# Splitting the first activation load and moving one residual add from TensorE to VectorE in a transformer block

## The chip, the cores and the metric

The kernel runs on one core of one Trainium2 chip. The metric is the device time of one execution in microseconds; several executions are timed and the median is given. The profile's span is about 1.7 us shorter than the timed execution, and spans are compared only with spans. The engines are TensorE (PE in the profile, its weight loads PEld), VectorE (DVE), ACT, GpSimd (POOL) and SP, whose queue issues 46 of the 50 transfers of the kernel before.

## The reference, cut to what matters

```python
x = A_x                                   # 2048 x 512, bf16
xn = _layernorm(x)                        # per row
# A: 32 heads of 16, causal attention over a window of 256 keys; then @ wo
# B: ((xn @ w_gate) * (xn @ w_up)) @ w_down, inner width 1792
return x + A(xn) + B(xn)
```

The sum of the three terms is the point: attention's output projection and the down projection accumulate in the same bank of PSUM, the memory that this kernel's matmuls write to, and the residual x is added last. Copying a finished bank out of PSUM is called evacuating it.

## The kernel before

Rows are worked off in four chunks of 512 (T = 0 to 3), each of four blocks of 128 rows. The first chunk is loaded and normalised ahead of everything:

```python
        for lo, hi in ((0, 1), (1, 4)):                      # x blocks 0, then 1 to 3
            nc.sync.dma_start(out=self.x[:, lo:hi, :], in_=xv[:, lo:hi, :])
        for lo in (1024, 512, 0):                            # V, K, Q thirds
            nc.sync.dma_start(out=self.Wqkv[:, :, lo:lo + 512], in_=wq[:, :, lo:lo + 512])
        ...
        for _ in range(38):                                  # the author's warm-up; no run isolates it
            nc.tensor.matmul(wps[:], lhsT=ident[:], rhs=ident[:], start=True, stop=True)
```

The rest is one hand-made list scheduler. Attention proceeds in groups of scores; between the groups "fillers" (all the dense matmuls, in pairs) are emitted until a running count of cost reaches the group's share of the total:

```python
        total = sum(w[0] for w in work) - RESERVE + SCORES * len(steps) + VALUES * (len(due) - 1)
        ...
        for g, s in enumerate(steps):
            fill(-1, g)
            self.scores(*s)                   # matmuls, then ACT's exponential, then GpSimd's masks
            ...
            upto = total * (g + 1) / len(steps)
            ...
                fill(upto, g)                 # fillers until the share is used up
                self.mask_diag(*s)
```

Every `scores` ends with up to four masks on GpSimd, which need the exponential. And a filler without matmuls, of cost 0, prepares a new chunk's V tile on GpSimd:

```python
    def new_chunk(self, T):
        ...
        nc.gpsimd.memset(self.heads(self.V[T])[:, :, :, 16:18], 1.0)   # the column of ones
        nc.gpsimd.memset(self.V[T][:, VW - 16:], 0.0)
        nc.gpsimd.memset(self.VS[T][:, SW - 16:], 0.0)

        def project(T):                       # in the list of fillers
            add(0, lambda: self.new_chunk(T))
            for b in range(4):
                for ks in halves:
                    add(2, lambda t=4 * T + b, ks=ks: self.proj_v(t, ks), ...)
```

The softmax here doesn't subtract the row's maximum and nothing guards it: scores larger than these inputs give would overflow.

## Time and profile before

| What | Before |
|---|---|
| time, median of 3 | 268.93 us |
| span of the profile | 267.5 us |
| TensorE busy | 258.4 us, 97% |
| VectorE, ACT, GpSimd busy | 68%, 64%, 43% |
| second norm statistics start | 4.80 us |
| first V projection matmul | 7.49 us |
| last evacuation on VectorE starts | 263.79 us |

The timeline of the kernel before at the start, with the last evacuation as its end; columns are start, length (both us), engine, line, operation, tiles, count, and in brackets the idle time before it and what ended it.

```profile
2.86 0.69 DVE L148 BATCH_NORM_STATS2 st<-x 128x6 f32<-128x512 bf16 x1 [1.02 <-DMA x<-in_A_x_dram]
4.80 0.70 DVE L148 BATCH_NORM_STATS2 st<-x 128x6 f32<-128x512 bf16 x1 [0.84 <-DMA x<-in_A_x_dram]
7.49 0.81 PE L200 MATMUL vp<-Wqkv,xnT 128*128 128x512 bf16 x3
263.79 0.56 DVE L402 TENSOR_TENSOR y<-L,x 128x384 bf16<-128x384 f32 x1 [2.47 <-PE L L384]
```

VectorE waits 0.84 us for blocks 1 to 3. Everything else in the norm follows in VectorE's order, so the wait is paid once by the whole kernel: in the chain that ended last, the load's 3.52 us (from 1.25 us) are followed by VectorE's norm work and from 8.43 us by TensorE. The count x3 stands for four matmuls: 22 matmul records are missing, so counts and busy time of TensorE are a little low.

### The profile page before, as it was taken

How to read it: one execution, taken by the hardware profiler on the slowest of the kernel's cores; microseconds unless marked ns; L12 is line 12 of the kernel's file. 1: busy time of each engine (PE TensorE's matmuls, PEld its weight loads, DVE VectorE, ACT ScalarE, POOL GpSimd, SP SyncE). 2: the span in 40 equal slices, each digit the busy share in tenths (PEclk: the TensorE clock that was granted, in tenths of full speed). 3: DMA queues.
4: the chain of work that ended last, by engine and by line, in shares of the span. 5: the costliest groups of instructions: out<-in, count | busy, mean ns of one | idle time of the engine just before them, and what ended most of it. 6: DMA issues, size and time to landing. Idle time of an engine off the chain costs nothing.

```text
span 267.5 us, 8861 instructions
## 1 busy us (share of the span) xinstructions
PE 258.4 (97%) x3860; PEld 119.1 (45%) x3882; DVE 181.7 (68%) x352; ACT 170.6 (64%) x132; POOL 113.8 (43%) x281
## 2 busy tenths in 40 slices
PE   6899999999999999999999999999999999999994
PEld 6444434444444444444444444444444444434453
DVE  4377898958756859676674868857762575978251
ACT  2675658696556776769656676668765667665500
POOL 5215333422674533345556433545444353443500
PEclk9999999999999999999999999999999999999999
DMA  6999911120023000001014100000200010000002
GB/s 205 373 358 334 250 22 22 23 47 0 4 61 81 20 2 4 2 2 44 5 23 97 43 0 5 0 4 2 44 5 20 26 39 2 2 0 2 4 2 81
DMA packets 19336, 15.13 MB, mean 57 GB/s; under 512 B 7264, under 2 KB 19296, under 8 KB 19296
## 3 DMA queue, kind: packets, MB, share of 16 engines
q1 hardware_dynamic: 18464, 14.09, 18.1%
q8 instruction: 30, 0.49, 0.7%
q10 hardware_dynamic: 832, 0.46, 0.6%
q14 instruction: 10, 0.08, 0.1%
HBM read 9.70 MB, written 2.10 MB: 44 GB/s over the span
## 4 chain that ended last, share of the span: by engine, by line
PE 88%; DVE 7%; issue 1%; DMA 1%; ACT 1%; SPq 0%; POOL 0%; DVEq 0%; POOLq 0%
PE up L359 17%; PE gp L345 17%; PE psd L378 16%; PE qkp L212 11%; PE S L261 9%; PE acc L316 6%; PE psd L384 5%; PE vp L200 4%; PE L L378 2%; DMA x<-in_A_x_dram 1%; DVE hT L363 1%; DVE st L148 1%; DVE at L322 1%; DVE gsb L353 1%; DVE xn L168 1%
## 5 line engine op out<-in xcount | busy, mean ns | idle before, releaser
L268 ACT ACTIVATE P<-S 128x2048 bf16<-128x2048 f32 x76 | 141.0, 1855 | 57.4 <-PE S L261 49.9
L137 POOL TENSOR_SCALAR_AFFINE_SELECT P<-P 64x256 bf16<-64x256 bf16 x224 | 97.3, 434 | 128.9 <-ACT P L268 118.2
L345 PE MATMUL gp<-xnT,Wg 128*128 128x512 bf16 x224 | 60.0, 380 | 0.1
L359 PE MATMUL up<-xnT,Wu 128*128 128x512 bf16 x224 | 59.6, 380 | 0.0
L378 PE MATMUL psd<-Wd,hT 128*128 128x512 bf16 (+1 forms) x198 | 48.7, 368 | 1.4 <-issue 1.3
L363 DVE TENSOR_TENSOR hT<-up,gsb 128x512 bf16<-128x512 f32 x56 | 38.4, 686 | 16.0 <-PE up L359 14.4
L289 DVE TENSOR_TENSOR P<-P,diag 128x512 bf16<-128x512 bf16 (+1 forms) x76 | 30.6, 404 | 10.4 <-ACT P L268 10.4
L322 DVE STREAM_TRANSPOSE at<-acc 128x512 f32<-128x512 f32 x30 | 19.7, 695 | 19.7 <-PE acc L316 19.7
L378 PEld LDWEIGHTS <-hT 128*128 128x128 bf16 x238 | 21.6, 98 | 25.3 <-issue 2.6
L359 PEld LDWEIGHTS <-Wu 128*128 128x128 bf16 x224 | 20.4, 98 | 25.3 <-issue 2.5
L345 PEld LDWEIGHTS <-Wg 128*128 128x128 bf16 x224 | 20.3, 98 | 25.5 <-issue 2.7
L261 PE MATMUL S<-Q,K 16*64 16x320 bf16 (+1 forms) x720 | 31.2, 260 | 0.4
L261 PE MATMUL S<-Q,Ko 32*64 32x320 bf16 (+1 forms) x720 | 31.1, 260 | 0.0
L212 PE MATMUL qkp<-xnT,Wqkv 128*128 128x512 bf16 x128 | 30.0, 380 | 0.0
L261 PEld LDWEIGHTS <-K 16*64 16x64 bf16 x720 | 12.2, 103 | 32.2 <-issue 32.2
L353 DVE CAST gsb<-gp 128x512 bf16<-128x512 f32 x36 | 24.5, 681 | 2.6 <-PE gp L345 1.3
L351 ACT ACTIVATE gsb<-gp 128x512 bf16<-128x512 f32 x20 | 11.9, 597 | 11.8 <-PE gp L345 11.1
L316 PE MATMUL acc<-P,VS 64*32 64x320 bf16 (+4 forms) x672 | 18.9, 254 | 0.0
L316 PE MATMUL acc<-P,V 64*32 64x320 bf16 (+4 forms) x672 | 18.4, 254 | 0.1
L212 PEld LDWEIGHTS <-Wqkv 128*128 128x128 bf16 x128 | 11.7, 98 | 14.5 <-issue 1.4
L384 PE MATMUL psd<-Wo,OT 128*128 128x512 bf16 (+1 forms) x55 | 15.5, 368 | 0.6 <-issue 0.6
L316 PEld LDWEIGHTS <-V 64*32 64x32 bf16 x720 | 14.5, 90 | 2.8 <-issue 2.4
(55 smaller groups left out, 194.1 us busy)
## 6 DMA issues: line engine op xcount, KB each, us to landing
Wg<-in_B_w_gate_dram SPq DMA_DIRECT2D x2, 896.0 KB, 10.4
Wu<-in_B_w_up_dram SPq DMA_DIRECT2D x2, 896.0 KB, 13.0
Wd<-in_B_w_down_dram SPq DMA_DIRECT2D x1, 1792.0 KB, 17.3
out_dram<-y SPq DMA_DIRECT2D x14, 128.0 KB, 1.8
Wqkv<-in_A_wqkv_dram SPq DMA_DIRECT2D x3, 512.0 KB, 6.4
x<-in_A_x_dram SPq DMA_DIRECT2D x1, 1024.0 KB, 10.9
VS<-V SPq DMA_DIRECT2D x6, 144.0 KB, 2.6
x<-in_A_x_dram SPq DMA_DIRECT2D x1, 512.0 KB, 11.4
```

Of the source, the lines that this page charges most:

```text
L137: nc.gpsimd.affine_select(out=v, in_=v, pattern=pattern + [[1 if diag else -1, 64]], compare_op=ALU.is_ge if diag else ALU.is_gt, fill=0.0 ...
L212: nc.tensor.matmul(ps[:], lhsT=self.Wqkv[:, k, lo:lo + 128], rhs=self.xnT[T][:, :, k, :], start=(k == 0), stop=(k == 3))
L261: nc.tensor.matmul(S[64 * par:64 * par + 64, e, col:col + n], lhsT=(self.Ko if par else self.K)[U][rows, c, keys], rhs=self.Q[T][rows, c, ...
L268: nc.scalar.activation(out=P[:, :, 0:col], in_=S[:, :, 0:col], func=ACT.Exp, scale=0.25)
L289: self.nc.vector.tensor_tensor(out=v, in0=v, op=ALU.min, in1=self.diag.unsqueeze(1).unsqueeze(1).to_broadcast([128, 4, n, 64]))
L316: nc.tensor.matmul(accs[par][32 * e:32 * e + 32, q:q + n], lhsT=v, rhs=P[rows, e, col:col + n], start=(i == 0), stop=(i == len(todo) - 1), ...
L345: nc.tensor.matmul(ps[:], lhsT=self.Wg[:, k, 128 * f:128 * f + 128], rhs=self.xnT[T][:, :, k, :], start=(k == 0), stop=(k == 3))
L353: nc.vector.tensor_copy(out=self.gsb[:], in_=ps[:])
L359: nc.tensor.matmul(ps[:], lhsT=self.Wu[:, k, 128 * f:128 * f + 128], rhs=self.xnT[T][:, :, k, :], start=(k == 0), stop=(k == 3))
L363: nc.vector.tensor_tensor(out=self.hT[T][:, f, :], in0=ps[:], in1=self.gsb[:], op=ALU.mult)
L378: nc.tensor.matmul(ps, lhsT=self.hT[T][:, f, 128 * b:128 * b + 128], rhs=self.Wd[:, f, c0:c1], start=(f == 0), stop=False)
L384: self.nc.tensor.matmul(ps, lhsT=self.OT[T][:, c, 128 * b:128 * b + 128], rhs=self.Wo[:, c, c0:c1], start=False, stop=(c == 3))
```

## The change

The intent has two parts. At the front, x block 1 gets its own transfer, so that its norm need not wait for 384 KB. At the end, the last chunk's second block no longer receives its x by an identity matmul and a copy on ACT; VectorE adds x while it evacuates the bank, as for most other blocks.

```diff
-        for lo, hi in ((0, 1), (1, 4)):
+        for lo, hi in ((0, 1), (1, 2), (2, 4)):
             nc.sync.dma_start(out=self.x[:, lo:hi, :], in_=xv[:, lo:hi, :])
@@ the last chunk's fillers
             if b < 3:
                 wo(T, b, (0, 1, 2))
-            if b in (1, 3):
-                add(1, lambda b=b: self.add_x(T, b, 0 if b == 1 else 1))
+        add(1, lambda: self.add_x(T, 3, 1))
@@ the tail
             self.wo(T, b, (3,))
-            self.store(T, b, on_act=(b == 1))
+            self.store(T, b)
```

## The prediction

> **What bounds the kernel now.** TensorE. The page gives PE 258.4 us busy of a 267.5 us span (97%), against DVE 68%, ACT 64%. The table of busy time by stretches shows PE at 9.6 to 10.0 of every 10 us from 10 to 260 us, at full granted clock. The exceptions are both ends. In the chain of waits the first large piece is the load of x blocks 1 to 3 (from 1.25 us, 3.52 us), then VectorE's norm work; only from 8.43 us is the chain TensorE's. At the end PE stops at 263.8 us; evacuation, store and closing take 3.5 us.
>
> **Front.** The timeline shows x block 0 landing at 2.85 us (2.0 us after issue) and VectorE through with its statistics at 3.95 us, then idle 0.84 us until blocks 1 to 3 (384 KB) land and the second statistics start at 4.80 us. The later norms follow in VectorE's order. After the change block 1 (128 KB) is issued at 1.2 us and, at block 0's 2.0 us, lands near 3.3 us. [...] Second statistics can start at 3.97 us, 0.83 us earlier; the third at 5.1 us if blocks 2 and 3 have landed. The same 512 KB passes, so I estimate 4.7 to 5.1 us: hardly a wait. Weights are issued 0.4 us later: the V third of Wqkv (issue 1.72 us, landing 4.5 us later, at 6.2) would come by 6.2 to 6.6 us; the first V matmul, now at 7.49 us, wants it at 6.65. The other weights have slack. TensorE's unbroken stretch begins 0.6 to 0.85 us earlier and keeps that. Estimate: 0.7 us.
>
> **End.** One 128x512 identity matmul goes: 0.216 us in an unbroken stream (four merged span 1.03 us, one alone 0.379). It lies on a full engine: 0.2 us. The add moves to VectorE, 0.68 us instead of ACT's 0.60, where VectorE is idle from 261.3 to 263.8 us: its three stores are done by 262.1 us, before the last evacuation. Four stores issue on SP instead of three, 0.4 us each, also done in time. No cost.
>
> **Moved without appearing in the diff.** One filler fewer lowers the scheduler's total, so from the second chunk on some pairs of matmuls cross a scores group and some evacuations change engine (gate copies on ACT 20 to 21, on VectorE 36 to 35; K copies on ACT 4 to 3). On engines at 64 to 68% I take this as noise of up to 0.3 us either way. [...]
>
> **Prediction.** 268.93 - 0.7 - 0.2 = 268.0 us, range 267.6 to 268.5. Faster by over 2%: 1%; within 2%: 98.5%; slower: 0.5%.
>
> **What would show each step.** Second statistics at about 4.0 us with hardly a wait for x; third at 5.1 us; first V matmul at 6.7 us; QK projection at 10.9 to 11.1 us instead of 11.74; PE's last matmul at about 262.9 us; no ACT store at 260 us; the tail after it still 3.5 us.
>
> **What would make it wrong.** Blocks 2 and 3 landing after 5.3 us, or Wv after 6.7 us: front gain 0.3 us or less. Reordered fillers opening waits of TensorE on scores or PSUM banks: the gain is eaten. The VectorE store delaying the last evacuation: a wait before the 128x384 store.

0.7 us for the front and 0.2 us for the end, 268.93 - 0.7 - 0.2 = 268.03 us, given as 268.0.

## More of the kernel before

```profile
181.14 2.76 PE L200 MATMUL vp<-Wqkv,xnT 128*128 128x512 bf16 x11
181.19 0.33 POOL L118 MEMSET V<- 128x256 bf16 x1
181.34 1.88 ACT L268 ACTIVATE P<-S 128x2048 bf16<-128x2048 f32 x1 [1.16 <-PE S L261]
183.12 1.57 ACT L204 ACTIVATE V<-vp 128x512 bf16<-128x512 f32 x3
183.29 1.99 POOL L137 TENSOR_SCALAR_AFFINE_SELECT P<-P 64x256 bf16<-64x256 bf16 x4 [1.68 <-ACT P L268]
184.55 1.91 ACT L268 ACTIVATE P<-S 128x2048 bf16<-128x2048 f32 x1
185.07 1.89 PE L212 MATMUL qkp<-xnT,Wqkv 128*128 128x512 bf16 x8
```

The memset at 181.19 us is done long before ACT's first copy of V at 183.12 us, and TensorE goes from V's projection to scores and on to the Q and K projection without a wait.

`proj_v` takes one of four rotating PSUM banks (`ps_m`), and ACT copies the result into V, behind the memset. The score tile S has one buffer only.

## The result, and the profile after

The changed kernel takes 270.29 us (median of 4, 270.00 to 270.41), the kernel before 268.96 us in the same rounds. The ratio is 1.005 (95% interval 1.0033 to 1.0067). Ratios here are taken over the fast runs of the same rounds, so they are not quite the ratio of the medians quoted. 1.3 us were lost where 0.9 us were to be gained, a miss of 2.3 us. That the forecast "within 2%" held says little: any loss of less than 5 us would have met it.

The front did what was intended. Timeline of the changed kernel at the start:

```profile
3.89 0.68 DVE L148 BATCH_NORM_STATS2 st<-x 128x6 f32<-128x512 bf16 x1
5.01 0.69 DVE L148 BATCH_NORM_STATS2 st<-x 128x6 f32<-128x512 bf16 x1
6.93 0.88 PE L200 MATMUL vp<-Wqkv,xnT 128*128 128x512 bf16 x3
```

The second statistics start at 3.89 us with no wait for x, and the first V matmul 0.56 us earlier. The loss must lie later. The list of what TensorE waited for, of the changed kernel (instruction and line, what it waited for, then us in total, times, longest), finds it:

```profile
PE qkp L212 <- ACT V L204: 1.2, 1, 1.2
PE S L261 <- ACT P L268: 0.9, 1, 0.9
```

Neither line is in that list of the kernel before. Each wait happened once. The busy time by stretches shows where: the columns are the stretch, its length, then busy time and instruction count of PE, PEld, DVE, ACT and POOL, the granted clock, the DMA share and GB/s. First the kernel before:

```profile
180.00:192.00 12.00, 11.95 (x127) 4.98 (x127) 8.87 (x18) 9.88 (x11) 5.64 (x15) 1.00 0.12 26
```

Then the changed kernel:

```profile
180.00:192.00 12.00, 9.88 (x117) 4.20 (x118) 6.07 (x11) 8.36 (x9) 4.73 (x13) 1.00 0.12 26
```

TensorE lost 2.07 us here, at full clock. The timeline of the changed kernel in that stretch:

```profile
180.41 2.76 PE L200 MATMUL vp<-Wqkv,xnT 128*128 128x512 bf16 x11
180.61 1.88 ACT L268 ACTIVATE P<-S 128x2048 bf16<-128x2048 f32 x1 [0.72 <-PE S L261]
182.55 2.09 POOL L137 TENSOR_SCALAR_AFFINE_SELECT P<-P 64x256 bf16<-64x256 bf16 x4 [2.59 <-ACT P L268]
184.70 0.33 POOL L118 MEMSET V<- 128x256 bf16 x1
185.06 1.57 ACT L204 ACTIVATE V<-vp 128x512 bf16<-128x512 f32 x3 [2.57 <-POOL V L118]
185.71 1.89 PE L212 MATMUL qkp<-xnT,Wqkv 128*128 128x512 bf16 x8 [1.21 <-ACT V L204]
186.51 1.90 ACT L268 ACTIVATE P<-S 128x2048 bf16<-128x2048 f32 x1
188.46 0.30 PE L261 MATMUL S<-Q,K 16*64 16x256 bf16 x4 [0.86 <-ACT P L268]
```

Read it as a chain. The memset now stands behind four masks in GpSimd's queue, and those wait for an exponential that ends at 182.49 us. GpSimd is not busy before that: it idles 2.59 us, with a ready memset behind a mask that is not (in the run early_memset below GpSimd runs no memset between 175 and 190 us: it is done before, so its buffer is free by then). The masks take 2.09 us, the memset runs at 184.70 instead of 181.19 us, and ACT's copies of V begin at 185.06 instead of 183.12 us. By then V's projections, whose last matmul ends at 184.50 us, hold all four banks of `ps_m`, so TensorE waits 1.21 us for the first to come free. The next exponential stands behind three copies in ACT's queue and starts 1.96 us later than before (186.51 against 184.55 us); as S has one buffer, TensorE waits another 0.86 us for it.

Neither engine let a ready instruction pass in this trace: GpSimd idled 2.59 us ahead of the masks with the memset behind them, and ACT idled 2.57 us ahead of the copies of V with the exponential behind them, whose scores had ended by 183.53 us.

Why did the memset move? The removed identity matmul was a filler of cost 1. Without it `total` is lower by 1, every group's share `upto` a little lower, and at one boundary the cost-0 filler `new_chunk` no longer fits before the scores, but only after them. Working the scheduler's sums through shows how narrow it was: the cost spent so far was 754.55 in both kernels, against a share of 754.62 before the change and 753.92 after it. The built instruction order of GpSimd confirms it. Before:

```
TensorScalarAffineSelect P_3663   (x2)
Memset V3      <- here
Memset V3, Memset VS3
TensorScalarAffineSelect P_3817   (x4, wait for the exponential)
```

After, with other buffer numbers:

```
TensorScalarAffineSelect P_3661   (x2)
TensorScalarAffineSelect P_3810   (x4, wait for the exponential)
Memset V3      <- here
Memset V3, Memset VS3
```

At the end, the three full-width stores on VectorE and the four transfers on SP cost nothing: the last evacuation waits for TensorE alone, as before. It comes at 265.14 us:

```profile
265.14 0.56 DVE L402 TENSOR_TENSOR y<-L,x 128x384 bf16<-128x384 f32 x1 [1.87 <-PE L L384]
```

The sum closes. From the first V matmul to this evacuation the kernel before took 263.79 - 7.49 = 256.30 us, the changed one 265.14 - 6.93 = 258.21 us: 1.91 us more, which is the 2.07 us of waits less 0.2 us for the identity matmul, within 0.1 us.

### The profile page after: what moved, and what is told of

Read it like the earlier page. It is cut to its first block, busy times and chain, and to the rows that moved or that the text cites. A ratio compares the mean times of both kernels' runs of the same rounds, so it can differ in the third digit from the quotient of the medians.

```text
span 268.7 us, 8864 instructions
## 1 busy us (share of the span) xinstructions
PE 259.0 (96%) x3860; PEld 119.5 (44%) x3881; DVE 182.2 (68%) x353; ACT 170.0 (63%) x131; POOL 113.7 (42%) x281
## 4 chain that ended last, share of the span: by engine, by line
PE 87%; DVE 6%; issue 2%; ACT 1%; POOL 1%; DMA 1%; POOLq 0%; DVEq 0%
PE up L359 17%; PE gp L345 16%; PE psd L378 16%; PE qkp L212 10%; PE S L261 9%; PE acc L316 6%; PE psd L384 5%; PE vp L200 4%; PE L L378 2%; DVE hT L363 1%; DVE st L148 1%; POOL P L137 1%; DVE gsb L353 1%; DMA x<-in_A_x_dram 1%; DVE at L322 1%
## 5 line engine op out<-in xcount | busy, mean ns | idle before, releaser
L353 DVE CAST gsb<-gp 128x512 bf16<-128x512 f32 x35 | 23.9, 682 | 3.0 <-PE gp L345 2.0
L351 ACT ACTIVATE gsb<-gp 128x512 bf16<-128x512 f32 x21 | 12.5, 597 | 12.1 <-PE gp L345 10.7
L384 PE MATMUL psd<-Wo,OT 128*128 128x512 bf16 (+1 forms) x57 | 16.1, 369 | 0.3 <-issue 0.3
L220 DVE CAST K<-qkp 128x512 bf16<-128x512 f32 x13 | 8.9, 686 | 10.3 <-PE qkp L212 10.3
```

The costliest lines, as they stand in the source:

```text
L353: nc.vector.tensor_copy(out=self.gsb[:], in_=ps[:])
L384: self.nc.tensor.matmul(ps, lhsT=self.OT[T][:, c, 128 * b:128 * b + 128], rhs=self.Wo[:, c, c0:c1], start=False, stop=(c == 3))
```

## The experiments

Theory A is the chain above: the loss sits in one place and comes from the memset's place in GpSimd's queue. The rivals: B, the reordered fillers and the evacuations that changed engine cost many small waits; C, the additional transfer or the later weights cost it; D, VectorE's store at the end costs it.

The instruction orders of the builds were compared: x_split_only has the order of before on all engines but SP, tail_only and early_memset have the changed kernel's order on TensorE, VectorE and ACT, and before_memset_late differs from before on GpSimd only. All kernels gave correct results. The first four runs of the table were made on one chip, the last three on another, so each is compared with the kernel before of its own rounds.

| Run | Median us | Lowest to highest | Kernel before, same rounds |
|---|---|---|---|
| x_split_only | 268.46 | 268.26 to 268.60 | 268.94 |
| reserve35 | 268.08 | 267.98 to 269.14 | 268.94 |
| memset_dve | 267.94 | 267.81 to 268.52 | 268.94 |
| before_memset_late | 271.24 | 270.86 to 272.63 | 268.94 |
| tail_only | 270.71 | 270.42 to 270.92 | 268.85 |
| early_memset | 268.17 | 268.08 to 268.63 | 268.85 |
| early_x1act | 270.41 | 268.72 to 271.10 | 268.85 |

In the rounds of the first four, 3 of the 11 runs of the kernel before took 270.5 to 270.6 us, the others 268.8 to 269.0 us. They count as fast runs and widen the intervals, so medians are compared there. That level appeared at a mean granted clock of 1.0; what causes it is open, as no profile of such a run was kept. One candidate is untested: the time before the first clock record does not lower that mean (1.000 in the profile of the changed kernel, whose first record begins at 7.10 us), so it would not show a full clock that came later. 3.41 us at half clock, as recorded in early_x1act below, would cost 1.7 us (an estimate from that record), about the size of the gap. Two runs of before_memset_late, at 272.44 and 272.63 us, lie above its lowest by about as much.

**x_split_only: the front alone, in the kernel before.**

```diff
-        for lo, hi in ((0, 1), (1, 4)):
+        for lo, hi in ((0, 1), (1, 2), (2, 4)):
```

> The kernel before with only the split x load; the instruction order of all engines but the SP queue is that of before. Theory A (the loss sits in one place, the memset of V for the last chunk, which the reordered fillers put behind masks on GpSimd): 268.4 us, 0.6 us faster than before, with no wait of TensorE between 180 and 190 us. Rival C (the added DMA, its semaphore or its later weights cost the time): 269.5 us or more. First V matmul at 6.9 us in both.

Measured: 268.46 us, 0.48 us under the median of before, with no wait of TensorE after the first 7 us. The split load helps; rival C falls.

**reserve35: the whole change, with the old total.**

```diff
-        RESERVE = 36
+        RESERVE = 35
```

`RESERVE` is subtracted from the total, so this restores every share, and with them the old place of the memset, while both parts of the change stay.

> The changed kernel with RESERVE 35 for 36, so that the scheduler's total and with it the place of every filler up to the tail are those of before. Theory A: 268.15 us (0.6 us from the front and 0.2 us from the identity matmul), no wait of TensorE near 185 us. Rival D (the store on VectorE or its queue costs the time): 269.5 us or more. Rival B (the reordered fillers cost by many small waits and by the evacuations that changed engine) also says 268.15, so this run does not part A from B.

Measured: 268.08 us, as theory A said; in its table of stretches TensorE is busy 12.00 of the 12 us from 180 us:

```profile
180.00:192.00 12.00, 12.00 (x129) 5.13 (x129) 8.70 (x18) 10.44 (x10) 5.21 (x14) 1.00 0.12 26
```

VectorE's store is still there, so rival D falls. Against x_split_only it differs by the end of the change alone: 0.38 us by the medians. In the traces, from first V matmul to last evacuation, the difference is 0.22 us (256.08 against 256.30 us), close to the 0.216 us that the prediction took for the identity matmul.

**memset_dve: the changed kernel's order, the memsets out of GpSimd's queue.**

```diff
-        nc.gpsimd.memset(self.heads(self.V[T])[:, :, :, 16:18], 1.0)
+        eng = nc.vector if T == 3 else nc.gpsimd
+        eng.memset(self.heads(self.V[T])[:, :, :, 16:18], 1.0)
         (and so for the other two memsets)
```

> The changed kernel with its own filler order; only the three memsets of the last chunk are on VectorE and no longer in GpSimd's queue. Theory A: 268.2 us, 2.1 us faster than the changed kernel, the waits of 1.2 and 0.9 us near 185 us gone. Rival B (order and evacuation engines as such): it stays at 270.3 us. Rivals C and D: 270.3 us too.

Measured: 267.94 us. The reordered pairs and the changed evacuation engines are all still in this kernel, so rival B falls. Its table of stretches has no idle TensorE from 180 us:

```profile
180.00:192.00 12.00, 12.00 (x129) 4.99 (x128) 8.09 (x20) 10.54 (x11) 4.86 (x11) 1.00 0.12 26
```

The timeline of memset_dve (its lines are one number higher) shows the memset 1.88 us earlier than in the changed kernel, while GpSimd's masks run beside it:

```profile
182.82 0.27 DVE L119 MEMSET V<- 128x256 bf16 x1
183.00 1.91 POOL L138 TENSOR_SCALAR_AFFINE_SELECT P<-P 64x256 bf16<-64x256 bf16 x4 [2.59 <-ACT P L269]
183.17 1.58 ACT L205 ACTIVATE V<-vp 128x512 bf16<-128x512 f32 x3 [0.24 <-DVE VS L121]
184.78 1.89 PE L213 MATMUL qkp<-xnT,Wqkv 128*128 128x512 bf16 x8
```

**before_memset_late: nothing of the change, only the memset moved.**

```diff
     def new_chunk(self, T):
         ...
-        (the three memsets)
+        if T == 3: self.owed = T
+        else: self.ones(T)                  # the three memsets
     def scores(self, T, c, pieces):
         ...                                 # after the masks of the group
+        if self.owed is not None:
+            self.ones(self.owed); self.owed = None
```

> The kernel before with one move only: GpSimd's three memsets for the last chunk issued after the four masks of the next scores group rather than ahead of them. Nothing of the change is in it. Theory A: 271.0 us, 2.1 us slower than before, with a wait of TensorE on V's evacuation of 1.2 us and one on the exponential of 0.9 us near 185 to 189 us. Rivals B, C and D: 268.96 us, unchanged.

Measured: 271.24 us, 2.3 us slower than before by the medians and 2.06 us by the lowest runs of each. The list of TensorE's waits of this kernel (lines seven higher) has the changed kernel's two:

```profile
PE qkp L219 <- ACT V L211: 1.1, 1, 1.1
PE S L268 <- ACT P L275: 0.9, 1, 0.9
```

So the move of three memsets past four masks is enough to make the loss, and by reserve35 and memset_dve, where it is undone and the loss is gone, it is needed for it.

**tail_only: the end of the change alone.**

```diff
-        for lo, hi in ((0, 1), (1, 2), (2, 4)):
+        for lo, hi in ((0, 1), (1, 4)):
```

> The changed kernel with its x load put back to one transfer for blocks 1 to 3: only the end of the change, with the reordered fillers. Theory A (V's memset behind the masks): 268.95 + 2.1 - 0.2 = 270.8 us, the two waits near 185 us there. If the loss came from the split load instead: 268.75 us.

Measured: 270.71 us, with both waits in the list of tail_only:

```profile
PE qkp L212 <- ACT V L204: 1.2, 1, 1.2
PE S L261 <- ACT P L268: 0.9, 1, 0.9
```

The half of the change that looked the simplest, one matmul fewer, brought the whole loss.

**early_memset: a version whose memset does not depend on that boundary.**

```diff
         def project(T):
-            add(0, lambda: self.new_chunk(T))
         ...
         def gu(T, between):
+            if T + 1 < NCH:
+                add(0, lambda: self.new_chunk(T + 1))
             for f in range(NF):
```

> The changed kernel, all orders of TensorE, VectorE, ACT and SP as they are; GpSimd's three memsets for a new chunk are issued a whole chunk's gate phase earlier. Theory A: 268.1 us like the run with the memsets on VectorE, no wait of TensorE near 185 us. Rival E (VectorE's memsets helped by something else than leaving GpSimd's queue): 270.3 us.

Measured: 268.17 us, ratio to before 0.9979 (0.9967 to 0.9991), no wait in the middle:

```profile
180.00:192.00 12.00, 12.00 (x131) 4.91 (x117) 7.69 (x16) 10.34 (x10) 5.00 (x12) 1.00 0.12 26
```

VectorE has no additional work here, so rival E of the expectation falls too. reserve35, memset_dve and early_memset all beat both kernels, by 0.7 to 1.0 us against before. The runs do not rank them: their medians, of different rounds and chips, lie within 0.23 us of each other.

**early_x1act: block 1 issued from ACT's queue, in the hope of earlier weights. A failure.**

```diff
         for lo, hi in ((0, 1), (1, 2), (2, 4)):
-            nc.sync.dma_start(out=self.x[:, lo:hi, :], in_=xv[:, lo:hi, :])
+            (nc.scalar if lo == 1 else nc.sync).dma_start(out=self.x[:, lo:hi, :], in_=xv[:, lo:hi, :])
         (and the edit of early_memset)
```

> As early_memset, and x block 1 is issued from ACT's queue at about 0.8 us instead of third in SP's, so that the weights are issued 0.4 us earlier, as in the kernel before. If the weights' later issue holds the first V matmul in the changed kernel (6.9 us; 7.3 us with a wait on Wqkv in the run with memsets on VectorE), it now starts by 6.65 us and the time is 267.9 us, 0.2 us under early_memset. If only VectorE's norms and the clock's warming hold it, no difference over 0.1 us.

Measured: 270.41 us, from 268.72 to 271.10 us: slower, and far less steady. The timeline of early_x1act:

```profile
3.61 0.69 DVE L148 BATCH_NORM_STATS2 st<-x 128x6 f32<-128x512 bf16 x1 [1.77 <-DMA x<-in_A_x_dram]
8.05 1.64 PE L200 MATMUL vp<-Wqkv,xnT 128*128 128x512 bf16 x4 [0.59 <-DMA Wqkv<-in_A_wqkv_dram]
```

In this profile block 0 came at 3.6 instead of 2.85 us (2.8 to 3.1 us in the other eight profiles), and the V weights 6.2 us after their issue at 1.72 us, although they were issued as early as in the kernel before, where they took 4.5 us. So the expectation failed on both sides of its "if": the issue came earlier and the landing later. The profile of this run also shows a lower granted clock just there, in the table of stretches of early_x1act:

```profile
8.00:10.00 2.00, 1.95 (x9) 1.04 (x10) 0.60 (x2) 0.31 (x2) 0.84 (x2) 0.58 1.08 385
10.00:12.00 2.00, 2.00 (x11) 0.90 (x9) 0.00 (x0) 1.02 (x3) 0.00 (x0) 0.57 1.06 383
```

Four matmuls took 1.64 us where the changed kernel's stream takes 1.03 us for four. The trace's own clock record is sharper than these averages: half the full clock from 8.32 to 11.73 us. From 6 to 8 us TensorE was busy only 0.67 of 2 us. Whether that sparse stretch caused the fall is not shown. Against the profile of early_memset, this one starts the first V matmul 1.41 us later (8.05 against 6.64 us) and takes 1.73 us longer from there to the last evacuation (257.63 against 255.90 us). But only two of the six runs (270.94, the profiled one, and 271.10 us) show a mean clock of 0.994; 270.15 and 270.67 us came at 1.0 and have no profile. Why the transfers came late with two queues is open.

## Why the prediction was wrong, point by point

- **What bounds the kernel: right.** TensorE is the bound (97% busy before), and where the middle stayed unbroken the front's gain arrived.
- **Front: right in mechanism, too large in size.** The second statistics came at 3.89 us (predicted 4.0) and the third at 5.01 us (5.1). The term "0.7 us" measured 0.48 us in the run that has only this part.
  - What there was to win: the prediction took VectorE's wait of 0.84 us from one profile, of a run of 269.22 us, slower than the timed median. The other two profiles with the unsplit load, before_memset_late and tail_only, show 0.38 and 0.56 us, and their first V matmul starts at 7.08 and 7.30 instead of 7.49 us. There was less to win.
  - What was won: in the five profiles with the split load issued on SP the first V matmul started at 6.59, 6.64, 6.76, 6.93 and 7.31 us; the last had a wait of 0.4 us on Wqkv, the case "Wv after 6.7 us" that the prediction named.
  - What the prediction left out: the 38 warming matmuls and the clock. The matmuls end at 5.67 us in some profiles (before, after) and 5.07 us in others (x_split_only), having taken 4.24 and 3.64 us: in the changed kernel's profile the transposes, ready since 5.1 us, came after them, and four took 0.63 instead of 0.40 us. The tables of stretches print a clock of 1.00 where the trace has no clock record yet. The first record, at full clock, begins at 4.28 us in x_split_only, at 6.27 and 6.33 us in early_memset and reserve35 and at 7.10 us in the changed kernel; in these four profiles every group of four transposes that starts before it takes 0.61 to 0.63 us, and those after it 0.39 or 0.40 us. The third statistics start within 0.01 us of each other in x_split_only and the changed kernel, the first V matmul 0.34 us apart, so this much goes with the late clock, though no run isolates it. Over the nine profiles the first record at full clock begins between 4.26 us (tail_only) and 7.10 us (the changed kernel).
- **End: right.** "0.2 us" for the identity matmul measured 0.22 us in the traces (0.38 us by the medians), and VectorE's store cost nothing.
- **Moved without appearing in the diff: this step failed.** The prediction saw the reordering and wrote "On engines at 64 to 68% I take this as noise of up to 0.3 us either way." It was 2.07 us, from two waits of TensorE in one place: 1.21 us for a PSUM bank and 0.86 us for the score tile. It listed the moves on TensorE, VectorE and ACT, and not the one on GpSimd, the least busy engine at 43%, though the two builds' order of GpSimd, shown above, has that move. Busy share says how much room an engine has on average; it does not say what stands behind what in its queue. The last paragraph did name "waits of TensorE on scores or PSUM banks" as a way to be wrong, which is what happened, but gave it no weight in the range.
- **The additional transfer.** It cost nothing that x_split_only could show: 0.48 us under the median of before, and no wait of TensorE after the first 7 us.

## What to carry to other kernels

Where a list scheduler shares work out by a total, removing any item can move what follows: compare the built instruction order of every engine, idle ones too, and ask of each instruction that changed places what now stands in front of it and what waits behind it. Zero-cost preparation, such as a memset that a later copy needs, is safer far ahead of its use than on a boundary where one unit of cost decides whether it precedes or follows an instruction that waits. After a change that should gain and does not, the list of TensorE's waits with a count of one is a good first place to look; here it held the whole loss in two lines.
